# Row sums of squares of the unpacked attention: two accumulated matmuls per block of rows instead of one matmul after an addition on GpSimd

## The chip, the cores and the metric

The kernel runs on one core of a Trainium2 chip. The metric is the device time of one execution in microseconds (us). The engines named here are TensorE (PE, with its weight loads shown apart as PEld), VectorE (DVE), ScalarE (ACT), GpSimd (POOL) and SyncE (SP), which here issues the DMAs.

## The reference

Three layers in a row. The first is an attention in two steps through 32 packed positions, for 8 batches, 8 heads, 576 positions and a head dimension of 64; then come two dense blocks on the 4608 rows of 512 values that result.

```python
def sm_attn(qq, kk, vv):                       # softmax(scale * qq kk^T) vv
    ...
p_packed = sm_attn(p, k, v)                    # 32 packed rows per head
out = sm_attn(q, p_packed, p_packed)           # 576 rows per head
x = out.transpose(0, 2, 1, 3).reshape(B * S, H * D)
rms = np.sqrt(np.mean(x * x, axis=-1, keepdims=True) + 1e-06)
xn = x / rms * rms_g
g = xn @ w_gate
h1 = (g / (1 + np.exp(-g))) * (xn @ w_val) @ w_out
a = h1 @ w1
b = h1 @ w2
return (a * b @ w3) @ w_out2
```

What the change touches is `rms`: the mean over 512 values of the square of each of the 4608 rows of `x`.

## The kernel before

The kernel works in float32 throughout; the large matmuls run on a high and a low part of each operand (`split`), three products to each.

**Stages.** For each batch b, `pack(b)` makes the packed rows, `unpack(b)` makes the second softmax and the scale of each row, and `dense_units` multiplies the result by the gate and value weights. The attention output `x` is never formed. `unpack` keeps the 576 softmax rows of all heads transposed, in `a2T`: 128 partitions (32 packed positions of 4 heads) by two halves `e = 0, 1` by 576 positions. The sum of squares of a row of `x` is then a quadratic form: line 343 multiplies `a2T` by `G`, the products of the packed rows with each other, line 348 multiplies the result by `a2T` element by element into `sq` (128 x 2 x 576), and the sum of `sq` over its partitions and over both halves is the sum of squares of each position. For batches 1 to 7, line 352 first adds the two halves on GpSimd, in place into `sq[:, 0]`. Lines 357 to 360 then sum over the partitions with TensorE: for each of R = 5 blocks of 128 positions, a matmul with a 128 x 128 block of `sq` as the stationary operand and `ones` (128 x 2, holding 1/512) as the moving one. Batch 0 has no addition; it issues two accumulating matmuls for each block, one for each half. Each such float32 matmul stands in the trace as two weight loads and two matmul records.

Line 361 (VectorE) reads the sums from PSUM and adds 1e-6, line 364 (GpSimd) raises them to the power -0.5, line 369 (TensorE) turns them into rows, line 371 (VectorE) scales `a2T`, and `split` (lines 59 and 60) makes `ah` and `al`, which the dense matmuls of the next batch read at line 432.

**Order.** Each engine takes its instructions in the order in which the program emits them, and that order is written out by hand (`manual_schedule`). `planned` walks over the dense units of batches 0 to 6, 48 steps to a batch, and calls one step of a generator at the step numbers given: `UNPACK` lists those of `unpack(b + 1)`, `PACK` those of `pack(b + 2)`, and so on. In the batches that `UNPACK` serves, the second multiplication of line 348 is emitted at step 24, the addition of line 352 at step 25, the matmuls of line 359 with line 361, and then line 364, at step 30, and the transposes of line 369 at step 35. A dense step is six matmuls into one of four PSUM banks (`bank`, tag "gv"); lines 438, 439, 444 and 447 read the bank, lines 444 and 448 make `ht`, and line 409 stores it. `unpack` and `wb_unit` (line 391) share two PSUM buffers (`slot("at")`). The conversion of the 64-bit weight words (lines 113 to 123) runs among all this on ScalarE, VectorE and GpSimd. After batch 7's dense units (up to about 490 us) follow the output projection, the weights of the second block and its matmuls, where none of the touched lines run.

Of the kernel before, what the change touches and what calls it, by code (L numbers as in the profile page):

```python
# [13 lines left out]
ALU = mybir.AluOpType  # L14
# [18 lines left out]
def packed_attention_swiglu_bilinear(ctx: ExitStack, tc, qT, kT, v, v_end, pT, rms_g, w_gv, w_out,  # L33
                                     w1, w2, w3T, w_out2, out):
    nc = tc.nc
# [248 lines left out]
    def unpack(b):  # L284
# [13 lines left out]
        for a, t in enumerate(ts):  # L298
            for c in range(NC):
                for e in range(2):  # L300
# [4 lines left out]
                                     start=True, stop=True, tile_position=(64 * e, r))  # L305
# [29 lines left out]
        sq = att.tile([128, 2, S], F32, tag="sq", name="sq")  # L335
        ts = [slot("at") for _ in range(2)]
        for a in range(2):
            for e in range(2):
                for c in range(NC):
# [5 lines left out]
                                     start=True, stop=True, tile_position=(k, r))  # L345
        over.add(("G", b))
        for e in range(2):
            nc.vector.tensor_tensor(out=halves(sq[:, e]), in0=ts[e][:, :, :HALF], in1=halves(a2T[:, e]),
                                    op=ALU.mult)
            yield  # L350
        if b:
            nc.gpsimd.tensor_tensor(out=sq[:, 0], in0=sq[:, 0], in1=sq[:, 1], op=ALU.add)
        yield
        ssq = att.tile([128, R], F32, tag="ssq", name="ssq")
        rinv = att.tile([128, R], F32, tag="rinv", name="rinv")
        t = slot("at")
        for r in range(R):
            for e in range(1 if b else 2):
                nc.tensor.matmul(t[:, 0, 2 * r:2 * r + 2], lhsT=sq[:, e, T0[r]:T0[r] + 128], rhs=ones,  # L359
                                 start=(e == 0), stop=(e == 1 or b > 0), skip_group_check=True)  # L360
        nc.vector.tensor_scalar(out=ssq, in0=t[:, 0, :2 * R].rearrange("p (r j) -> p r j", j=2)[:, :, 0],
                                scalar1=0.0, scalar2=1e-6, op0=ALU.max, op1=ALU.add)
        yield
# [155 lines left out]
    def spin():  # L519
        while True:  # L520
            t = bank()
            for _ in range(4):
                nc.tensor.matmul(t[:, :128], lhsT=ident, rhs=ident, start=True, stop=True)
            yield

    gens = dict(x=spin(), p=pack(0), u=unpack(0), c=gvw, d=gvd, w=wb_first(), l=later(), P=pack(1), U=unpack(1),
                Q=pack(2), V=unpack(2), R=pack(3), o=ow)
    for x in ("pxxpxdxcxppdpcdpccdxcuduudcxuldupuxcuuw"
              "xxxxxdxlcuxxxxxxdcuuduuuPxlPPluPuxuuPldP"):
# [16 lines left out]
    for b in range(2, B - 1):  # L546
        if b + 2 < B:
            steps.append(([48 * b + n for n in PACK], pack(b + 2)))
        steps.append(([48 * b + n for n in UNPACK], unpack(b + 1)))
        steps.append(([48 * b + n for n in WOUT], ow))  # L550
# [560 lines left out]
```

## Time and profile before

| | us |
|---|---|
| Median of 3 runs | 1348.25 (1348.1 to 1349.21) |
| The profiled execution | 1346.48 |
| Its span, first to last instruction | 1344.6 |
| TensorE busy | 1322.6 (98%) |
| VectorE busy | 875.4 (65%) |
| ScalarE busy | 577.7 (43%) |
| GpSimd busy | 557.4 (41%) |

The mean granted clock of TensorE over the span is 0.996 of full speed.

A profile records one execution. Busy time is what an engine spent in instructions; the ends of pipelined matmuls are modelled, and some matmul records can be missing, so a busy TensorE may still hold short waits. The chain follows the work that ended last backwards, at each step to what released it. An entry such as "A <- B: 2.7, 4" says that A's engine sat idle four times, 2.7 us in all, until B was done. Spans on GpSimd are rough.

### The profile page before, as it was taken

The numbers are of one execution on the slowest core, as the hardware profiler recorded it, in microseconds if no ns is written. First come the engines' busy times: TensorE is split into PE (matmuls) and PEld (weight loads), VectorE is DVE, ScalarE is ACT, GpSimd is POOL, SyncE is SP. The second block draws the span as 40 slices with busy tenths as digits, with TensorE's granted clock in tenths as the row PEclk, the third lists the DMA queues.
The fourth block names the chain that finished last, engine by engine and source line by source line (L and its number), as shares of the span: only waits on it lengthen the run. The fifth ranks groups of instructions, "written<-read, shape, count | busy, mean of one in ns | idle before, by whom it ended". The sixth has DMA issues, their size and how long they took to land.

```text
span 1344.6 us, 23644 instructions
## 1 busy us (share of the span) xinstructions
PE 1322.6 (98%) x9010; PEld 1124.2 (84%) x9010; DVE 875.4 (65%) x1286; ACT 577.7 (43%) x1117; POOL 557.4 (41%) x467
## 2 busy tenths in 40 slices
PE   7989999999999999999999999999999999999998
PEld 6768888888888888888888888888888888899998
DVE  5796677777776557727475664578459657657645
ACT  5645566667666655525243442124015103305113
POOL 3341446656556542203221313445345335435442
PEclk9989999999999999999999999999999999999999
DMA  9855467647342576724399885656755856787875
GB/s 342 305 187 199 152 219 255 218 160 265 125 160 104 166 243 225 241 81 156 107 379 388 316 278 210 223 209 225 263 203 200 287 187 219 249 299 262 282 272 185
DMA packets 88706, 304.04 MB, mean 226 GB/s; under 512 B 9872, under 2 KB 14992, under 8 KB 74384
## 3 DMA queue, kind: packets, MB, share of 16 engines
q1 hardware_dynamic: 88592, 302.52, 63.9%
q8 instruction: 71, 1.16, 0.4%
q14 instruction: 43, 0.35, 0.1%
HBM read 223.87 MB, written 76.55 MB: 223 GB/s over the span
## 4 chain that ended last, share of the span: by engine, by line
PE 88%; DVE 7%; DMA 2%; issue 2%; ACT 1%; POOL 0%; SPq 0%; DVEq 0%; ACTq 0%; POOLq 0%
PE gv L432 21%; PE gv L946 13%; PE at L946 13%; PE at L636 12%; PE gv L636 7%; PE gv L1040 5%; PE at L1040 5%; PE at L391 3%; PE gv L736 3%; DVE sl L60 1%; PE at L214 1%; DVE wbl L60 1%; PE at L343 1%; PE at L245 1%; PE at L359 1%
## 5 line engine op out<-in xcount | busy, mean ns | idle before, releaser
L448 POOL TENSOR_TENSOR ht<-th,vl 128x288 f32<-128x288 f32 x168 | 138.9, 836 | 121.2 <-ACT vl L447 68.9
L432 PE MATMUL gv<-ah,wbh 128*128 128x288 f32 x768 | 174.5, 308 | 4.6 <-DVE th L439 3.9
L432 PEld LDWEIGHTS gv<-ah,wbh 128*128 128x128 f32 x768 | 121.2, 188 | 55.9 <-issue 22.5
L432 PE MATMUL gv<-al,wbh 128*128 128x288 f32 x768 | 164.7, 295 | 0.0
L432 PE MATMUL gv<-ah,wbl 128*128 128x288 f32 x768 | 164.1, 295 | 0.0
L60 DVE TENSOR_TENSOR hl<-hr,hh 128x512 fp32r<-128x512 f32 x108 | 101.3, 943 | 75.1 <-ACT hh L59 72.9
L972 POOL TENSOR_TENSOR s<-uc 128x512 f32<-128x512 f32 (+1 forms) x40 | 49.0, 1224 | 231.6 <-DVE uc L928 231.6
L946 PE MATMUL gv<-xh,w 128*128 128x512 f32 (+1 forms) x560 | 137.8, 367 | 0.0
L946 PE MATMUL at<-xh,w 128*128 128x512 f32 (+1 forms) x560 | 137.7, 367 | 0.0
L123 POOL TENSOR_TENSOR c_o<-c_o,c_y 128x512 int32<-128x512 int32 x52 | 71.0, 1366 | 146.2 <-DVE c_o L121 124.8
L439 DVE SCALAR_TENSOR_TENSOR th<-th,gv 128x288 f32<-128x288 f32 x192 | 84.9, 445 | 61.6 <-ACT th L438 52.4
L432 PEld LDWEIGHTS gv<-al,wbh 128*128 128x128 f32 x768 | 123.4, 188 | 0.0
L432 PEld LDWEIGHTS gv<-ah,wbl 128*128 128x128 f32 x768 | 123.3, 188 | 0.0
L59 ACT ACTIVATE hh<-hr 128x512 fp32r<-128x512 f32 x108 | 67.6, 629 | 115.2 <-PE at L636 60.1
L946 PEld LDWEIGHTS gv<-xh,w 128*128 128x128 f32 x560 | 102.5, 188 | 13.4
L946 PEld LDWEIGHTS at<-xh,w 128*128 128x128 f32 x560 | 102.5, 188 | 13.3
L636 PE MATMUL at<-hl,wo_h 128*128 128x512 f32 x288 | 112.1, 389 | 0.0
L636 PE MATMUL at<-hh,wo_l 128*128 128x512 f32 x288 | 112.1, 389 | 0.0
L636 PE MATMUL at<-hh,wo_h 128*128 128x512 f32 x288 | 112.0, 389 | 0.0
L438 ACT ACTIVATE th<-gv 128x288 f32<-128x288 f32 x192 | 78.7, 410 | 53.2 <-PE gv L432 51.8
L447 ACT ACTIVATE vl<-gv 128x288 f32<-128x288 f32 x168 | 69.2, 412 | 50.1 <-PE gv L432 35.1
L60 POOL TENSOR_TENSOR xl<-yi,xh 128x1024 fp32r<-128x1024 f32 (+1 forms) x20 | 57.3, 2872 | 74.0 <-ACT xh L59 49.9
(164 smaller groups left out, 2836.1 us busy)
## 6 DMA issues: line engine op xcount, KB each, us to landing
w<-ws_d SPq DMA_DIRECT2D x40, 1024.0 KB, 5.0
w<-w_d SPq DMA_DIRECT2D x35, 1024.0 KB, 4.8
w<-ws_d SPq DMA_DIRECT2D x40, 768.0 KB, 4.6
hT_d<-ht SPq DMA_DIRECT2D x96, 288.0 KB, 3.5
hr<-hT_d SPq DMA_DIRECT2D x108, 256.0 KB, 4.9
w<-in_w_gv_dram SPq DMA_DIRECT2D x24, 512.0 KB, 6.1
w<-in_w_out_dram SPq DMA_DIRECT2D x20, 512.0 KB, 5.0
q<-in_qT_dram SPq DMA_DIRECT2D x8, 1152.0 KB, 7.6
```

Of the source, the lines that this page charges most:

```text
L59: nc.scalar.activation(out=hi, in_=src, func=AF.Copy)
L60: eng_lo.tensor_tensor(out=lo, in0=src, in1=hi.bitcast(F32), op=ALU.subtract)
L123: nc.gpsimd.tensor_tensor(out=d, in0=d, in1=shape(y), op=ALU.add)
L432: nc.tensor.matmul(t[:, :HALF], lhsT=w[:, e, 256 * i + 128 * f:256 * i + 128 * f + 128], rhs=x[:, e, HALF * hf:HALF * hf + HALF], start=(n ...
L438: nc.scalar.activation(out=th, in_=t[:, :HALF], func=AF.Tanh, scale=0.5)
L439: nc.vector.scalar_tensor_tensor(out=th, in0=th, scalar=1.0, in1=t[:, :HALF], op0=ALU.add, op1=ALU.mult)
L447: nc.scalar.activation(out=vl, in_=t[:, :HALF], func=AF.Copy, scale=0.5)
L448: nc.gpsimd.tensor_tensor(out=ht[:, hf], in0=th, in1=vl, op=ALU.mult)
L636: nc.tensor.matmul(acc[m], lhsT=w[:, kk, 128 * m:128 * m + 128], rhs=x, start=(kk == 0 and a == 0), stop=(kk == NF - 1 and a == 2))
L946: nc.tensor.matmul(t, lhsT=wi[:, r, pos, a], rhs=x[:, j, r, :w], start=(start and at == 0), stop=(at == 5), skip_group_check=True)
L972: nc.gpsimd.tensor_tensor(out=s2, in0=u2, in1=c22, op=ALU.mult)
L1040: nc.tensor.matmul(t, lhsT=wi[:, s, k, 128 * m:128 * m + 128], rhs=x, start=(j in (0, 5, 4, 3) and k == 0 and n == 0), stop=(k == 3 and n ...
```

## The change

The addition on GpSimd at line 352 is taken out, and the matmuls of line 359 run over both halves in every batch, as they did in batch 0: two matmuls for each block of positions, the first starting the accumulation in PSUM and the second ending it. Nothing else is moved; the step of `unpack` that held the addition stays as an empty step.

```diff
-        if b:
-            nc.gpsimd.tensor_tensor(out=sq[:, 0], in0=sq[:, 0], in1=sq[:, 1], op=ALU.add)
         yield
         ssq = att.tile([128, R], F32, tag="ssq", name="ssq")
         rinv = att.tile([128, R], F32, tag="rinv", name="rinv")
         t = slot("at")
         for r in range(R):
-            for e in range(1 if b else 2):
+            for e in range(2):
                 nc.tensor.matmul(t[:, 0, 2 * r:2 * r + 2], lhsT=sq[:, e, T0[r]:T0[r] + 128], rhs=ones,
-                                 start=(e == 0), stop=(e == 1 or b > 0), skip_group_check=True)
+                                 start=(e == 0), stop=(e == 1), skip_group_check=True)
```

## Rows read from the trace of the kernel before

**Rows 1.** the profile's page: busy time by engine, then shares of the last-ending chain

```profile
PE 1322.6 (98%) x9010; PEld 1124.2 (84%) x9010; DVE 875.4 (65%) x1286; ACT 577.7 (43%) x1117; POOL 557.4 (41%) x467
...
PE 88%; DVE 7%; DMA 2%; issue 2%; ACT 1%; POOL 0%; SPq 0%; DVEq 0%; ACTq 0%; POOLq 0%
```

**Rows 2.** busy microseconds by stage; each row starts with the stretch and its length

```profile
core 0: us, PE busy (x) PEld busy (x) DVE busy (x) ACT busy (x) POOL busy (x), PEclk, DMA share, GB/s
...
48.00:100.00 52.00, 45.71 (x460) 35.97 (x460) 46.85 (x88) 30.82 (x60) 21.97 (x18) 0.93 0.66 234
100.00:490.00 390.00, 388.61 (x4123) 326.17 (x4122) 269.72 (x464) 246.55 (x550) 211.61 (x227) 1.00 0.54 184
490.00:1344.60 854.60, 850.49 (x3982) 732.29 (x3980) 529.63 (x683) 278.33 (x468) 305.40 (x199) 1.00 0.68 239
```

**Rows 3.** TensorE's own waits, 100 to 490 us: total us, times, longest us

```profile
PE at L230 <- ACT a1T L234: 0.8, 1, 0.8
```

**Rows 4.** the same for the weight loads, the largest entry

```profile
PEld gv L432 <- issue: 20.3, 30, 0.8
```

**Rows 5.** instructions of line 352 (GpSimd's addition): least, median, greatest ns

```profile
L352 POOL TENSOR_TENSOR sq<-sq x7: 1418/1601/1635, 94.0 to 418.6; 128x576 f32<-128x576 f32 x7
```

**Rows 6.** instructions of line 359 and what its engine waited for

```profile
L359 PE MATMUL at<-ones,sq x90: 165/251/272, 39.4 to 422.8; 128*128 128x2 f32 x90
L359 PEldq EVENT_SEMAPHORE  x6: 51/51/51, 95.1 to 371.7; - x6
...
  DVE sq L348: 2.7, 4
```

**Rows 7.** timeline, TensorE, batch 0: start us, us, engine, line, operation, count

```profile
40.05 2.17 PE L359 MATMUL at<-ones,sq 128*128 128x2 f32 x18 [0.28 <-DVE sq L348]
42.15 1.55 PE L214 MATMUL at<-k,pTs 64*32 64x288 f32 x32
```

**Rows 8.** timeline around line 359 in batch 2

```profile
158.89 1.17 PE L359 MATMUL at<-ones,sq 128*128 128x2 f32 x10
...
159.92 0.51 PE L432 MATMUL gv<-ah,wbh 128*128 128x288 f32 x2
```

**Rows 9.** timeline of batch 4, the addition and the sums

```profile
258.21 1.61 POOL L352 TENSOR_TENSOR sq<-sq 128x576 f32<-128x576 f32 x1
...
258.57 1.79 DVE L121 SCALAR_TENSOR_TENSOR c_o<-c_h,c_t 128x512 int32<-128x512 int32 x1
...
263.19 1.25 PE L359 MATMUL at<-ones,sq 128*128 128x2 f32 x10
...
263.77 0.69 DVE L121 SCALAR_TENSOR_TENSOR c_o<-c_h,c_t 128x512 int32<-128x512 int32 x1
...
264.29 0.52 PE L432 MATMUL gv<-ah,wbh 128*128 128x288 f32 x2
...
264.95 0.15 DVE L361 TENSOR_SCALAR ssq<-at 128x5 f32<-128x5 f32 x1
...
266.72 1.17 POOL L364 TENSOR_TENSOR rinv<-ssq,mhalf 128x5 f32<-128x5 f32 x1
...
268.36 0.71 PE L369 MATMUL at<-ident,rinv 128*128 128x128 f32 x5
```

**Rows 10.** timeline of batch 1, around its sums

```profile
96.00 1.17 PE L359 MATMUL at<-ones,sq 128*128 128x2 f32 x10
...
96.95 0.46 DVE L444 SCALAR_TENSOR_TENSOR ht<-th,gv 128x288 f32<-128x288 f32 x1 [1.89 <-DMA hT_d<-ht]
...
97.46 0.54 PE L432 MATMUL gv<-ah,wbh 128*128 128x288 f32 x2 [0.28 <-DVE ht L444]
...
98.61 1.28 POOL L123 TENSOR_TENSOR wgv<-wgv,c_y 128x512 int32<-128x512 int32 x1 [3.17 <-DVE wgv L121]
...
98.89 0.53 PE L432 MATMUL gv<-ah,wbh 128*128 128x288 f32 x2 [0.37 <-DVE th L439]
```

## The prediction

> **What bounds the kernel now.** The page's first part and its chain come first: TensorE is busy 98% of the span, and the chain that ended last runs through TensorE for 88% of it [rows 1]. The chip therefore has little else to wait for, but a mean over 1344.6 us does not say whether that holds where the change lies. Line 359 runs between 39.4 and 422.8 us [rows 6] and the addition between 94.0 and 418.6 us [rows 5], so the busy time by stage is the next view [rows 2]. The reader is to see three different stretches. From 48 to 100 us TensorE is busy 45.71 of 52 us while VectorE has 46.85: there the two change places as the bound. From 100 to 490 us TensorE is busy 388.61 of 390 us, so at most 1.4 us of idle time are there to be won or to be filled, and VectorE (269.72), ScalarE (246.55) and GpSimd (211.61) have over 100 us to spare. After 490 us, where no touched line runs, TensorE has 850.49 of 854.6 us. The granted clock is 1.00, its upper level of 2.4 GHz, in both later stretches. The waits view asks the same question in another way: in 100 to 490 us only one wait of TensorE has a releaser, 0.8 us for ScalarE's line 234 [rows 3]. The weight loads show longer idle entries, none over 0.8 us at a time; the largest sum of these, 20.3 us in 30 entries, is "issue", idle time with no releaser [rows 4]: the loader is ahead and the array is still streaming. Six of the seven batches that change lie in that stretch (2 to 7); batch 1 has its sums at 96 us, in the mixed one.
>
> **What is removed.** Seven additions on GpSimd, median 1.601 us [rows 5], so about 7 x 1.6 = 11.2 us of GpSimd's time. Nobody waited for them: the idle time before line 359 has one releaser in the whole trace, VectorE's line 348, 2.7 us in 4 entries [rows 6], and line 348 is the multiplication that stays (all four lie in batch 0, which has no addition; [rows 7] shows one of them). In batch 4 the addition ends at 258.21 + 1.61 = 259.82 us and line 359 starts at 263.19 [rows 9], 3.4 us later. Five dense steps stand between them in the emitted order, and these hide it. The cover is not lost, since the work itself is gone. In the place of the wait on GpSimd line 359 gets a wait on VectorE's line 348, emitted one step earlier, so it is met earlier still. The six 51 ns semaphore events ahead of line 359 [rows 6], one for a batch, may go with it; they stand in the loader's queue while the array works, so I count them at nothing, and at 6 x 0.05 = 0.3 us of gain at the most.
>
> On GpSimd the removal pulls forward what is queued behind the addition (lines 123 and 448), and with it the stores of line 409 on SP's queue. In the stretch that matters no wait of TensorE ends on GpSimd or a DMA [rows 3], so this is worth nothing by the rows, and at most the 1.4 us of idle time [rows 2].
>
> There is a second effect beside it, on VectorE. In batch 4 line 121 starts at 258.57, inside the addition, and takes 1.79 us; the same operation on the same shape takes 0.69 at 263.77 [rows 9]. Line 121 meets the addition in this way in five batches (3 to 7), so VectorE gets back about 5 x 1.10 = 5.5 us. VectorE has 390 - 269.72 = 120 us of idle time there [rows 2], and I count it at nothing.
>
> The Trainium skill, "SBUF — State Buffer", section "Who interferes with whom", says that VectorE reaches its second SBUF input through ports it shares with GpSimd, and that whichever instruction starts first holds them until it is done. The trace agrees in its direction: 1.79 against 0.69 us. By that rule alone the removal would look like a gain on both engines; the rival below works out what it gives if VectorE is the bound.
>
> **What is added.** In each of batches 1 to 7, five float32 matmuls more, each two loads and two matmul records: ten pairs on top of ten. The unit is not a record's 0.25 us [rows 6], since neighbours overlap. In batch 2 the ten pairs start at 158.89, and the next dense matmul starts at 159.92, 1.03 us later [rows 8]. In batch 4 the group takes 264.29 - 263.19 = 1.10 us [rows 9]. Batch 0 already does exactly what the change makes of the others: 18 of its pairs go from 40.05 to 42.15, so 2.10 / 18 = 0.117 us each [rows 7]. Ten more cost between 1.03 and 1.17 us. I take 1.13 us, about the middle of batch 4, whose pattern is that of four of the six batches, and batch 0, the only group that is as long as the new ones.
>
> In batches 2 to 7 this lies on the path: 6 x 1.13 = 6.8 us.
>
> In batch 1 it fills idle time. The present ten start at 96.00 and are through about 1.03 us later; TensorE then waits for VectorE's line 444, which itself had waited 1.89 us for a DMA, and starts again at 97.46. After that group of six matmuls it waits again, and starts the next at 98.89 [rows 10]. With ten more pairs the first restart is at 96.00 + 1.03 + 1.13 = 98.16, and the group takes about 0.80 us (six times the 0.13 us between dense matmuls), so the next could start at 98.96 instead of 98.89: 0.1 us lost. VectorE's and ScalarE's work on that group is late by 0.7 us meanwhile, so the bound upwards is the full 1.13, the bound downwards 0. I take 0.1. GpSimd in batch 1 sat idle 3.17 us before its next instruction at 98.61 [rows 10], so the missing addition pulls nothing forward there.
>
> **What is queued behind the longer group.** VectorE's line 361 waits for line 359, and behind it on VectorE stand the readers of the dense banks; GpSimd's line 364 and its successors come next. In batch 4 line 361 starts at 264.95 although line 359 was through at about 264.4, since VectorE came late; line 364 starts at 266.72, ends at 267.89, and line 369 on TensorE starts at 268.36 [rows 9], 0.47 us of margin. With the longer group, everything that hangs on the dense matmuls behind it moves by the same 1.13 us, line 369 included, while line 361 can start at about 265.6, that is 0.65 us later than now. The margin before line 369 grows rather than shrinks. I count nothing here. The price if the cover failed would be about another 1.1 us in each batch, in the rivals below.
>
> **The sum.** 6.8 + 0.1 = 6.9 us more. The profiled execution would go from 1346.48 to about 1353.4, its span from 1344.6 to 1351.5. The median of the runs stands 1.8 us above the profiled execution; I add to the median: 1348.25 + 6.9 = 1355.15, say 1355.2 us, 0.5% slower.
>
> **The rivals.**
>
> *Faster: GpSimd or VectorE sets the pace of the batches.* If the modelled ends of the matmuls hide waits, and TensorE in truth goes at GpSimd's pace, each batch from 1 to 7 gets shorter by the addition, and the added matmuls fall into the hidden waits: 1348.25 - 11.2 = 1337.1 us. It decides from the point at which such waits hold more than the added 1.13 us in a batch. For it speaks only that busy TensorE is not TensorE at its peak; against it GpSimd's 211.61 of 390 us [rows 2] and that no wait of TensorE ends on it [rows 3]. Chance 2%.
>
> *No difference: VectorE sets the pace, and its freed time pays.* If line 121's longer run is what the dense banks wait for in batches 3 to 7, its 5.5 us come off again: 1355.2 - 5.5 = 1349.7 us, within 0.2%. For it speaks the 1.79 us of line 121 [rows 9], against it VectorE's 120 idle us [rows 2] and the missing wait [rows 3]. This is the port rule of the page named above, and the trace shows its cause but not its effect on TensorE. Chance 4%.
>
> *More: the pace of line 359 is carried to its readers.* If lines 361, 364 and 369 become a chain that TensorE waits for, each batch pays 1.1 us twice: 1355.2 + 7 x 1.1 = 1362.9 us. Against it stands the margin just worked out. Chance 4%.
>
> *More: the added pairs don't overlap.* Then a pair costs its record's 0.25 us [rows 6], and the sum is 7 x 10 x 0.25 = 17.5 us: 1365.8 us. Both batch 0 and batch 2 speak against it [rows 7, 8]. Chance 2%.
>
> **How the numbers follow.** The forecast has 88%. Its own range: at the low end six batches at 1.03 us, nothing in batch 1, and the 1.4 us of idle time given back, 6.2 - 1.4 = 4.8; at the high end 7 x 1.17 = 8.2 us; the runs before differ by 1.1 us among themselves, so about 0.8 us more on each side: 1352.2 to 1357.3. The rivals outside it hold 12% together, less than the 20% to be left out, so the range stays there. The measurement tells apart about 0.2%, 2.7 us: slower is from 1350.95 us on. The forecast lies above that with all of its range; with the two dearer rivals that makes 94%. The same: 4%. Faster: 2%.
>
> **What would show it.** In the profile of the changed kernel line 359 has 160 matmul records instead of 90 (8 batches x 20), each of its groups in batches 2 to 7 takes about 2.2 us from its first start to the next dense matmul, and line 352 is gone. The end of the dense stage, now near 490 us, comes about 7 us later, and the rest of the span keeps its length. GpSimd's busy time falls by about 11 us and VectorE's by about 5.5, with line 121 at 0.69 us in all batches. TensorE's idle time from 100 to 490 us stays below 2 us. What would make the prediction wrong: a group that takes 1.5 us or less (the added pairs are cheaper), a dense stage whose other parts get shorter (the freed engines mattered), or waits of TensorE on lines 361, 364 or 439 that are new.

## The result and the profile after

| | before | changed |
|---|---|---|
| Median of the runs, us | 1348.17 (4 runs, 1347.98 to 1349.21) | 1360.59 (4 runs, 1358.29 to 1363.54) |
| Ratio to before, 95% interval | 1 | 1.0096 [1.0084, 1.0108] |
| The profiled execution, us | 1346.48 | 1358.29 |
| Its span, us | 1344.6 | 1356.5 |
| Mean granted clock of its span | 0.996 | 0.992 |

The change made the kernel about 12.4 us slower. The forecast was 6.9 us, and 1360.59 lies above the range that went with it. The sign and the place were right, the amount was not.

The page after, the lines that answer to [rows 1]:

```profile
PE 1334.9 (98%) x9080; PEld 1137.1 (84%) x9080; DVE 869.8 (64%) x1286; ACT 577.5 (43%) x1117; POOL 545.7 (40%) x460
...
PE 87%; DVE 7%; DMA 2%; issue 2%; ACT 1%; SPq 0%; POOL 0%; DVEq 0%; ACTq 0%; POOLq 0%
```

The busy time by stage, with the columns of [rows 2]. Lines of the program from 352 on carry numbers lower by two in the changed kernel: 357 is the old 359, 430 the old 432.

```profile
48.00:100.00 52.00, 46.36 (x463) 36.86 (x464) 46.69 (x87) 30.88 (x59) 21.64 (x17) 0.92 0.67 239
100.00:490.00 390.00, 388.57 (x4124) 327.61 (x4124) 259.49 (x456) 241.29 (x539) 195.91 (x216) 0.99 0.52 178
490.00:1356.50 866.50, 862.18 (x4048) 742.97 (x4046) 534.16 (x691) 283.27 (x480) 309.74 (x205) 1.00 0.67 238
```

The line of the sums, which answers to [rows 6], and the only wait of TensorE between 100 and 490 us, which answers to [rows 3]:

```profile
L357 PE MATMUL at<-ones,sq x160: 166/252/341, 39.5 to 434.2; 128*128 128x2 f32 x160
...
  DVE sq L348: 2.7, 4
```

```profile
PE at L230 <- ACT a1T L234: 0.8, 1, 0.8
```

All of this is as forecast. GpSimd is busy 11.7 us less (557.4 to 545.7) and VectorE 5.6 us less (875.4 to 869.8); line 357 has its 160 records; TensorE's idle time from 100 to 490 us is 1.4 us, as before; no wait of TensorE is new. TensorE is busy 12.3 us longer, though (1322.6 to 1334.9), where 70 more pairs at about 0.11 us make 7 or 8. One number differs where nothing should: the granted clock from 100 to 490 us is 0.99 and not 1.00.

The chain of the work that ended last shows where. Columns: start, duration, engine, line, count. First before, then after; the pieces are those behind the groups of sums.

```profile
160.06 2.49 PE gv L432 x18
...
209.00 1.11 PE at L359 x10
210.10 4.09 PE gv L432 x30
...
264.43 4.09 PE gv L432 x30
...
318.75 4.09 PE gv L432 x30
...
483.97 32.66 PE at L636 x144
```

```profile
98.51 3.95 PE gv L430 x18
...
162.87 4.03 PE gv L430 x18
...
213.51 2.15 PE at L357 x20
215.66 4.09 PE gv L430 x30
...
268.88 2.15 PE at L357 x20
271.03 5.62 PE gv L430 x30
...
327.90 4.09 PE gv L430 x30
...
495.27 32.66 PE at L634 x144
```

In batch 3 the group of twenty pairs takes 2.15 us where ten took 1.11, and the same 30 dense matmuls behind it take 4.09 us in both kernels. In batch 4 the group takes 2.15 us too, but the 30 dense matmuls behind it take 5.62 instead of 4.09. Behind batch 2, 18 dense matmuls take 4.03 instead of 2.49; behind batch 1, 18 take 3.95. The distance between the two kernels grows by these steps: the piece behind the sums of batch 3 starts 5.56 us later than before (215.66 - 210.10), batch 4's 6.60, batch 5's 9.15 (327.90 - 318.75), and the output projection 11.30 (495.27 - 483.97). Three pieces are 1.46 + 1.54 + 1.53 = 4.5 us too long (the 1.46 against batch 2's 2.49, since the kernel before has waits in batch 1). What is left, 11.30 - 4.5 = 6.8 us, fits the longer groups: in the same chain those of batches 2 to 7 grow by 1.04 to 1.12 us each, 6.45 us together. Of the other 0.35 us, 0.24 stand there ahead of batch 2's group (160.75 - 159.05 less the 1.46), about 0.1 of them before any group that changes.

The granted clock in those stretches, in the stage view of the changed kernel (it is the value before the last two), and one pair of dense matmuls inside and one ahead of such a stretch:

```profile
98.00:102.00 4.00, 4.00 (x20) 4.00 (x20) 1.22 (x4) 0.36 (x1) 1.99 (x2) 0.57 0.19 74
162.00:166.00 4.00, 4.00 (x23) 4.00 (x24) 0.84 (x3) 0.67 (x2) 2.55 (x3) 0.63 0.02 4
164.00:166.00 2.00, 2.00 (x11) 2.00 (x10) 0.00 (x0) 0.67 (x2) 1.11 (x2) 0.50 0.00 0
214.00:218.00 4.00, 4.00 (x34) 4.00 (x35) 1.46 (x5) 1.63 (x6) 3.13 (x3) 1.00 0.67 246
272.00:276.00 4.00, 4.00 (x21) 4.00 (x20) 0.92 (x2) 2.29 (x6) 2.97 (x4) 0.57 1.04 411
```

```profile
271.51 0.43 PE L430 MATMUL gv<-ah,wbl 128*128 128x288 f32 x2
...
273.75 0.68 PE L430 MATMUL gv<-ah,wbl 128*128 128x288 f32 x2
```

Behind batch 1 (98 to 102 us) the mean granted clock is 0.57, behind batch 2 (162 to 166) 0.63 and behind batch 4 (272 to 276) 0.57; behind batch 3 (214 to 218) it is 1.00. Inside such a stretch, from 164 to 166 us, it is 0.50, the lower level. The same two matmuls that pass in 0.43 us at 271.51 take 0.68 at 273.75. TensorE is busy for the whole of every row: by the profile it isn't waiting, it is slower. The clock has fallen from 2.4 to 1.2 GHz for a time right behind a group of sums, and a dense stretch that TensorE fills pays for that in full.

The kernel before had shown this already, in a place that the prediction used for another purpose. Its batch 0 has a group of twenty pairs, ending at 42.2 us. In the stage view of the kernel before:

```profile
40.00:44.00 4.00, 3.96 (x51) 3.15 (x52) 1.46 (x4) 0.00 (x0) 2.52 (x3) 0.94 0.99 409
44.00:48.00 4.00, 3.69 (x19) 3.22 (x19) 1.81 (x6) 2.63 (x6) 0.00 (x0) 0.63 0.11 46
48.00:52.00 4.00, 3.71 (x99) 3.26 (x99) 3.05 (x5) 2.89 (x7) 0.00 (x0) 1.00 0.32 88
```

Behind that group the clock stands at 0.63. Behind the seven groups of ten it never left 1.00.

### The profile page after: what moved, and what is told of

Same layout as the page of the kernel before. It is cut to its first block, busy times and chain, and to the rows that moved or that the text cites. A ratio compares the mean times of both kernels' runs of the same rounds, so it can differ in the third digit from the quotient of the medians.

```text
span 1356.5 us, 23772 instructions
## 1 busy us (share of the span) xinstructions
PE 1334.9 (98%) x9080; PEld 1137.1 (84%) x9080; DVE 869.8 (64%) x1286; ACT 577.5 (43%) x1117; POOL 545.7 (40%) x460
## 4 chain that ended last, share of the span: by engine, by line
PE 87%; DVE 7%; DMA 2%; issue 2%; ACT 1%; SPq 0%; POOL 0%; DVEq 0%; ACTq 0%; POOLq 0%
PE gv L430 22%; PE gv L944 13%; PE at L944 13%; PE at L634 12%; PE gv L634 7%; PE at L1038 5%; PE gv L1038 5%; PE at L389 3%; PE gv L734 3%; DVE sl L60 1%; PE at L357 1%; DVE wgv L121 1%; DVE wbl L60 1%; DVE c_t L120 1%; PE at L343 1%
## 5 line engine op out<-in xcount | busy, mean ns | idle before, releaser
L60 DVE TENSOR_TENSOR hl<-hr,hh 128x512 fp32r<-128x512 f32 x108 | 98.4, 917 | 77.0 <-ACT hh L59 73.0
```

The lines of the kernel that those rows point to most:

```text
L60: eng_lo.tensor_tensor(out=lo, in0=src, in1=hi.bitcast(F32), op=ALU.subtract)
```

## The experiments

The theory: an unbroken group of twenty pairs, all with a moving operand of two columns, is followed by a stretch of halved clock in some batches, about 1.5 us each, and the rest is the forecast's own 1.06 us or so for each group. The rivals: the pairs or their readers cost more than counted, or the missing addition does something on the other engines. Times below are medians; the ratios are to the kernel before as measured beside them, with 95% intervals (before: 1347.49 us for the first four, 1347.91 for the others).

**e1: the removal alone.** 

```diff
-        if b:
-            nc.gpsimd.tensor_tensor(out=sq[:, 0], in0=sq[:, 0], in1=sq[:, 1], op=ALU.add)
```

> The kernel before without the addition of line 352, and still with ten pairs (one half) in each of batches 1 to 7; the second half is left out of the sum of squares, so the row scales differ. Theory (nobody waits for the addition; all of the change's cost is in TensorE's longer group): the time of before, 1348.2 us within 0.1%, and the granted clock of TensorE at 1.00 from 100 to 490 us. Rival (taking the addition away moves GpSimd's and VectorE's work so that something new is late): a part of the 12 us shows here already, 1350 us or more. Second rival (the freed engines mattered): under 1347 us.

Measured: 1347.80 us, ratio 1.0001 [0.9992, 1.0010]. From 100 to 490 us:

```profile
100.00:490.00 390.00, 388.35 (x4127) 326.32 (x4127) 266.46 (x470) 246.95 (x551) 203.49 (x222) 1.00 0.54 183
```

No difference, and the clock at 1.00. The removed addition was worth nothing, and its absence harms nothing.

**e2: the added matmuls alone.** The loop over both halves in all batches, with the addition left in.

```diff
-            for e in range(1 if b else 2):
+            for e in range(2):
...
-                                 start=(e == 0), stop=(e == 1 or b > 0), skip_group_check=True)
+                                 start=(e == 0), stop=(e == 1), skip_group_check=True)
```

> The kernel before with its addition kept and both halves summed by TensorE as well (the second half is counted twice, so the row scales differ). Theory (the longer group costs about 1.06 us of work in a batch and, after some of the groups, a stretch of 3.4 us at half the granted clock, some 1.7 us each): as the changed kernel, 1358 to 1364 us, with at least one stretch at 0.5 between 100 and 490 us. Rival (the removed addition has a part in it): near 1355 us, 6 x 1.06 + 0.1 more than before, at a clock of 1.00.

Measured: 1360.79 us, ratio 1.0100 [1.0086, 1.0113]. By stage:

```profile
96.00:114.00 18.00, 17.82 (x122) 15.91 (x121) 9.80 (x21) 4.79 (x10) 4.21 (x4) 0.81 0.27 103
114.00:270.00 156.00, 154.81 (x1836) 127.96 (x1835) 107.73 (x193) 96.07 (x217) 76.36 (x83) 1.00 0.61 206
270.00:282.00 12.00, 12.00 (x91) 10.89 (x90) 6.18 (x13) 6.77 (x17) 7.18 (x8) 0.86 0.90 305
...
384.00:394.00 10.00, 10.00 (x76) 8.99 (x76) 4.09 (x9) 4.84 (x13) 6.80 (x7) 0.83 0.56 170
```

The whole loss is here without the removal, and the clock falls again: behind batch 1 (0.81 from 96 to 114 us), batch 4 (0.86 from 270 to 282) and batch 6 (0.83 from 384 to 394). Between batches 1 and 4 it stays at 1.00. Behind batch 1 the stretch is about twice as long as the others: the clock stands (1 - 0.81) x 18 = 3.4 us below full, against 0.14 x 12 = 1.7 and 0.17 x 10 = 1.7. So the groups it falls behind are not the same as in the changed kernel, although TensorE's instructions are.

**e3: the same twenty pairs, 96 columns wide.** Against the changed kernel, the moving operand is 128 x 96 instead of 128 x 2; all columns of a block hold the same sum, and line 361 reads the first.

```diff
+    wide1 = att.tile([128, 96], F32, name="wide1")
+    nc.gpsimd.memset(wide1, 1.0 / DM)
...
-                nc.tensor.matmul(t[:, 0, 2 * r:2 * r + 2], lhsT=sq[:, e, T0[r]:T0[r] + 128], rhs=ones,
+                nc.tensor.matmul(t[:, 0, 96 * r:96 * r + 96], lhsT=sq[:, e, T0[r]:T0[r] + 128], rhs=wide1,
...
```

> The changed kernel with a moving operand of 96 columns instead of 2, so the same twenty pairs keep the array streaming (the result is the same). Theory (the clock falls because the group of twenty pairs streams almost nothing): the granted clock stays at 1.00 from 100 to 490 us, a group takes 2.2 to 2.6 us (the 128-column transposes of line 230 pass at 0.13 us each), and the time is below that of the changed kernel although its matmuls are 48 times as wide: 1355 to 1358 us. Rival (the pairs themselves, or what they delay on other engines, cost the 12 us): 1361 us or more, since no pair gets cheaper.

Measured: 1353.99 us, ratio 1.0051 [1.0038, 1.0063], about 1 us below the range that was expected. Its stage from 100 to 490 us, and its chain at batches 3 and 4:

```profile
100.00:490.00 390.00, 388.55 (x4151) 327.20 (x4150) 262.71 (x463) 244.03 (x545) 200.10 (x220) 1.00 0.53 181
```

```profile
211.55 2.23 PE at L359 x20
213.77 4.01 PE gv L432 x30
...
266.90 2.23 PE at L359 x20
269.13 4.00 PE gv L432 x30
```

The matmuls are 48 times as wide, a group takes 2.23 us instead of 2.15, and the kernel is 6.6 us faster than the changed one. The clock is 1.00 throughout, and the 30 dense matmuls take 4.01 and 4.00 us in both batches. Nothing differs but the width and the columns that line 361 reads, so a price of the pairs themselves can't be what made up the difference.

**e4: the same pairs, dealt out.** Two columns again, but a `yield` behind each block of positions, so that dense matmuls stand between them. The step lists get the additional entries; for most batches:

```diff
+            if b and r < R - 1:
+                yield
...
-    UNPACK = [-1, -1, 0, 2, 7, 8, 12, 16, 16, 23, 24, 25, 30, 30, 35, 36, 38, 43]
+    UNPACK = [-1, -1, 0, 2, 7, 8, 12, 16, 16, 23, 24, 25, 30, 31, 32, 33, 33, 33, 36, 37, 38, 43]
...
```

> The changed kernel with the twenty pairs of a group dealt out over three or more neighbouring dense steps in batches 1 to 7, two or four or eight pairs in each, with lines 359 and 362 one to five steps later (the result is the same). Theory (it is the unbroken group of little streaming that lowers the clock): clock 1.00 from 100 to 490 us and 1348.2 + 6 x 1.06 + 0.1 to 0.5 = 1354.7 to 1355.5 us. Rival (the cost is per pair): 1360 us, as the changed kernel.

Measured: 1355.41 us, ratio 1.0066 [1.0052, 1.0080]. Its stage from 100 to 490 us, and a part of its timeline on TensorE in batch 3:

```profile
100.00:490.00 390.00, 388.51 (x4152) 326.96 (x4151) 258.97 (x460) 245.13 (x545) 200.06 (x219) 1.00 0.53 180
```

```profile
210.70 0.54 PE L357 MATMUL at<-ones,sq 128*128 128x2 f32 x4
211.10 0.52 PE L432 MATMUL gv<-ah,wbh 128*128 128x288 f32 x2
211.46 0.43 PE L432 MATMUL gv<-al,wbh 128*128 128x288 f32 x2
211.72 0.43 PE L432 MATMUL gv<-ah,wbl 128*128 128x288 f32 x2
211.99 0.50 PE L357 MATMUL at<-ones,sq 128*128 128x2 f32 x4
```

The clock is 1.00 over this stage in the profiled execution, and the median stands where the forecast stood. (Behind batch 0's group, which stays unbroken, it falls as before, to 0.57 from 44 to 48 us.) One of the six executions took 1359.83 us at a mean clock of 0.992 (0.995 or 0.996 in the others). No profile of that one exists, so where its clock fell is not known, and dealing out is not shown to rule the fall out.

**e5: the kernel before, with the wide operand.** The addition stays, ten pairs in batches 1 to 7, twenty in batch 0; the edit to line 359 is that of e3.

> The kernel before (addition kept, ten pairs in batches 1 to 7, twenty in batch 0) with a moving operand of 96 columns in line 359. In the trace of the kernel before the clock falls to half right behind batch 0's group of twenty (0.63 from 44 to 48 us) and nowhere behind the groups of ten. Theory (an unbroken group of twenty with little streaming is what lowers the clock): the fall behind batch 0 goes, the rest stays, and the time is that of before or up to 1.7 us less, 1346 to 1348 us. Rival (the wide operand brings something of its own, good or bad): more than 2 us away from before in either direction.

Measured: 1345.95 us, ratio 0.9989 [0.9980, 0.9998]: faster than the kernel before by about 1.5 to 2 us (0.3 to 2.7 by the interval), at the lower edge of what was expected, and the fastest here along with e7. Behind batch 0, and in the second place where the kernel before has a low clock:

```profile
44.00:48.00 4.00, 2.97 (x33) 2.11 (x20) 2.06 (x6) 2.41 (x6) 0.38 (x1) 1.00 0.22 90
...
84.00:88.00 4.00, 4.00 (x36) 2.23 (x37) 3.64 (x8) 2.04 (x3) 1.36 (x2) 0.50 0.93 263
```

The fall behind batch 0 is gone (1.00 instead of 0.63), as expected. The one at 84 to 88 us is still there.

**e6: e3 without batch 0.** The wide operand in batches 1 to 7 only.

```diff
...
+                                 rhs=wide1 if b else ones,
...
```

> The changed kernel with 96 columns in batches 1 to 7 and 2 columns in batch 0. Theory: the clock falls behind batch 0 as in the kernel before (about 44 to 48 us) and stays at 1.00 from 100 to 490 us; the time is that of the kernel before plus the added pairs alone, 7 groups, 6.5 to 7.5 us more, 1354 to 1355.5 us. Rival (e3's gain over the changed kernel came mostly from batch 0): 1358 us or more.

Measured: 1355.64 us, ratio 1.0066 [1.0054, 1.0079], a shade above the 1355.5 that was the upper end. Behind batch 0:

```profile
44.00:48.00 4.00, 4.00 (x40) 2.65 (x38) 1.63 (x5) 0.65 (x2) 1.19 (x1) 0.52 0.26 108
```

The clock is low there again (0.52); from 100 to 490 us it is 1.00. Against the kernel before beside it, e6 is 1355.64 - 1347.91 = 7.7 us slower, e3 1353.99 - 1347.49 = 6.5. Batch 0 may account for these 1.2 us, but the two intervals overlap. The larger part of e3's gain comes from the other seven batches: the changed kernel lost 12.4 us, e6 7.7, and their intervals don't overlap.

**e7: the other low stretch filled.** e5 with four calls of the existing idle matmuls in dense steps 19 to 22 of batch 0.

```diff
-            ("o", [22, 82])]
+            ("o", [22, 82]),
+            ("x", [19, 20, 21, 22])]
+    gens["x"] = some(gens["x"], 4)
```

> e5 with sixteen matmuls on the identity matrix dealt out over four dense steps of batch 0 (their result is not used), where TensorE is idle for 3.7 of 8 us between 76 and 84 us and the clock falls to half until 88 us in the kernel before. Theory (the fall there costs time, since TensorE is fully busy from 84 to 88 us at half clock): the clock stays up, and 0.5 to 2 us less than e5. Rival (VectorE sets the pace there, 3.6 to 3.96 of every 4 us busy, and the clock costs nothing): the same as e5, or more by the matmuls that don't fit into the gaps.

Measured: 1346.06 us, ratio 0.9989 [0.9980, 0.9998], the same as e5.

```profile
80.00:84.00 4.00, 2.98 (x28) 2.37 (x26) 3.93 (x9) 1.39 (x4) 1.66 (x2) 1.00 0.26 85
84.00:88.00 4.00, 3.89 (x46) 3.06 (x42) 3.82 (x8) 2.04 (x4) 1.64 (x2) 1.00 0.93 302
```

The clock now stays at 1.00 from 80 to 88 us, and the time doesn't move. My theory fell here and the rival held: VectorE is busy 3.93 and 3.82 of each 4 us, and in the chain of e7 all work from 76.1 to 87.2 us is VectorE's. The traces agree that nothing was won: in batch 1 the matmuls of line 393 start at 99.35 us instead of e5's 99.84, but the sums of batch 0, ahead of the edit, already start at 40.08 instead of 40.59. The low clock of this stretch cost no time.

**e8: the changed kernel once more.**

> The changed kernel once more, for a second profile. Theory (the clock falls behind some groups and not behind others, and not behind the same ones in each execution): the stretches at 0.5 between 96 and 490 us number 2 to 5 and stand behind groups of line 357, not all behind batches 1, 2 and 4 as in the first profile, and the time is 1354.8 us plus about 1.6 us for each. Rival (the place in the program decides): the same three.

Measured: 1358.46 us. In its chain, the dense matmuls behind the groups of batches 1 to 5:

```profile
98.45 4.03 PE gv L430 x18
...
163.27 4.03 PE gv L430 x18
...
215.85 4.09 PE gv L430 x30
...
271.24 5.61 PE gv L430 x30
...
328.13 4.09 PE gv L430 x30
```

The time is about 1 us below 1354.8 + 3 x 1.6 = 1359.6. The long pieces are behind batches 1, 2 and 4 again, so my expectation missed: this program showed the fall at the same three places in both profiled executions. What selects them stays open. The place in the program alone doesn't, since e2 has the same TensorE instructions and other places. The executions of the changed kernel lie between 1358.29 and 1363.54 us, the slowest at a mean clock of 0.989, so some probably held more or longer low stretches than the two that were profiled. The clock is not all that differs between executions: one of 1358.96 us has 0.994, the one of 1358.29 us 0.992.

## Why the prediction was right or wrong

**What bounds the kernel: right.** TensorE was the bound where six of the seven groups lie, and nothing absorbed the added time there.

**What is removed: right.** e1 is 1.0001 [0.9992, 1.0010]. GpSimd's 11.7 us and VectorE's 5.6 us came free as worked out (11.2 and 5.5), and bought nothing. The five instances of line 121 that took 1.79 us beside the addition are gone; the longest left in batches 3 to 7 take 1.30 and 1.17 us, so "0.69 us in all batches" was nearly right. The Trainium skill's rule of the shared ports ("SBUF — State Buffer", "Who interferes with whom") told rightly that VectorE would be released. e1 showed that nobody was waiting for it.

**The price of the pairs: right, within about 1 us.** I had 1.13 us for a group; in the chain batches 2 to 7 paid 1.04 to 1.12. In batch 1 the matmuls of line 389, the old 391, start at 102.46 us instead of 100.74; 1.46 of these 1.72 us are the low clock, which leaves 0.26 for the group and for a shift of about 0.1 that stood there before it, against the 0.1 of the sum. All seven together cost 6.6 to 6.8 us against 6.9. The kernels whose clock stayed up behind the groups of batches 1 to 7, e4 and e6, are 7.9 and 7.7 us slower than the kernel before beside them, a little more than the forecast.

**What is queued behind the longer group: right in the effect.** Line 359, the old 361, now waits 4.6 us in 7 entries for the sums, and no wait of TensorE came of it.

**The step that failed: the sum took every microsecond of TensorE at the clock of the kernel before.** The prediction read the granted clock, 1.00 in both later stretches [rows 2], and treated it as given. It is a result of what TensorE runs, and the change altered that: the term that is missing is three stretches at 1.2 GHz, 1.46 + 1.54 + 1.53 = 4.5 us in the profiled execution. With it the groups' 6.8 us come to the 11.3 us by which the output projection is late; the span grew by 11.9. (The last 0.5 or so arises later, at a wait for a load of line 565, the old 567, near 700 us; whether it belongs to the change is open.) None of the rivals was this mechanism. The two dearer ones, the pace carried to the readers (1362.9 us) and the pairs that don't overlap (1365.8 us), reached beyond the measured time, but for reasons that the runs don't show. A rival for the clock, worked out from the 1.5 us that each stretch cost here, would have had to reach to about 1348.2 + 6.9 + 7 x 1.5 = 1365.6 us.

**What should have been read.** I cited batch 0 as the one group that is "as long as the new ones" and read its pace from it [rows 7], but not the clock behind it: 0.63 from 44 to 48 us. The prediction looked at the clock by stage, as a mean, and the stage from 0 to 48 us didn't stand among its rows. The Trainium skill, "TensorE: Matmul & The Clock Gate", section "What's actually happening", says that the gate sets the clock by how busy TensorE has been of late. The trace agrees in part: the clock followed what TensorE ran, since the same pairs with 96 columns left it at 1.00 (e3). But it fell right behind the groups of twenty narrow pairs, to 0.63 and 0.57 in batches 2 and 4, while the profile shows TensorE busy all along, so the profile's busy share does not tell when it falls. I didn't weigh that rule, because the profile showed TensorE busy.

## What to carry to other kernels

A granted clock of 1.00 in the profile belongs to the instructions that ran: before adding many narrow matmuls in a row to a dense stretch, look for a group of that length that the kernel already has, and read the clock in the few microseconds behind it. Time freed on an engine that nobody waits for is worth nothing, and work moved from it onto the engine that bounds costs its full price. In these runs a low clock cost time only where TensorE set the pace (e7 against the changed kernel). Where it did, a wider operand in the same weight loads was the best cure tried (e3, e5), though it does not make this change a gain: e3 is still 6.5 us slower than the kernel before.

## What the runs showed of the hardware

With the moving operand 96 columns wide instead of 2, a group of twenty float32 pairs took 2.23 us instead of 2.15. The extra columns were nearly free (the narrow groups of e2 took 2.13 to 2.23 us in batches 2 to 7). Behind the wide groups the granted clock stayed at 1.00; behind the narrow ones it was 0.57 to 0.63 in the three stretches shown. The clock fell behind only three of the seven groups in each profiled execution, and behind different ones in two kernels with the same TensorE instructions. The kernel before with the wide operand in line 359 (e5) is, with e7, the fastest version found: 1345.95 us, ratio 0.9989 [0.9980, 0.9998].
